# Attention and channel mix on one core: the table of ranks that sets the issue order, written anew

## The chip, the cores and the metric

The kernel runs on one core of a Trainium2 chip. The metric is the device time of the whole program in microseconds (us); lower is better. Five engines work side by side, each through its own queue in the order in which the program was written: TensorE (PE in the profile, with its weight loads as PEld), VectorE (DVE), ScalarE (ACT), GpSimd (POOL) and SyncE (SP), which here issues every DMA.

## The reference

Attention over 8 batches of 8 heads, 576 positions and 64 features per head, with a rotary turn of queries and keys; then a channel mix over the 512 joined features.

```
q_rot, k_rot = rotate(q), rotate(k)
attn = softmax(q_rot @ k_rot.T / sqrt(64))
x = attn @ v                                  # heads joined: 8 x 576 x 512
xk = mu_k * x + (1 - mu_k) * x_prev           # x_prev: one position earlier
xr = mu_r * x + (1 - mu_r) * x_prev
k = relu(xk @ w_k) ** 2                       # 512 -> 1024
out = sigmoid(xr @ w_r) * (k @ w_v)           # 1024 -> 512
```

## The kernel before

**Work.** The 64 heads go in 32 pairs (`PAIRS`, numbered 0 to 31 here; four pairs are one batch). For each pair the kernel loads queries, keys (`xq`, `xk`) and values. The rotary turn (`plan_rope`) is two multiplications by a table and a sum, on DVE or POOL (tiles `xq`, `xk`, line 276). For pairs 4 to 31 the result is split into a high part (`qh`, `kh`) and the rest (`ql`, `kl`), and a product is three matmuls (line 440); pairs 0 to 3, the early pairs, use one product in full precision. `plan_unit` makes scores in five column steps per pair, here written S9.2 for step 2 of pair 9: the products into PSUM (`scores`, two slots for pairs 4 to 31), a maximum on DVE (`nm`, L451), the exponential on ACT (`pe`, L461) and a transpose of 32x32 blocks on DVE (`p`, L466). `plan_move` sends `p` to DRAM (`turned`) and back (`rows`); the early pairs are transposed on PE instead (`turn`, L486, copied to `rows`). `plan_values` multiplies `rows` by the values (`av`, L558: 40 matmuls in the trace for a pair) and DVE divides by the sums into `xT` (L565, L570).

When four pairs of a batch are done, `plan_channel_mix` works on that batch in two halves of 288 positions. `plan_mix` makes eight mixed inputs: `mxf` on ACT and DVE (L615, L620), then `mxh` and `mxl`, its high part and rest. The products (`acc`, L644 to L646) are groups of three matmuls of 128x288: key products with `wk` (i runs over the four pairs of the batch), gate products with `wr`, value products with `wv` on the squared keys `kkh`, `kkl`. The weights arrive as 64-bit words in 20 blocks (`raw`) and are converted once on ACT, DVE and POOL (L317 to L330), with high parts and rests (`wk_h`, `wk_l`, ...).

**What sets the order.** Nothing is written out by hand. Each operation is handed to `Plan.op` with the engines that can do it, a cost for each, what it must come after, and a rank. `Plan.issue` plays the program through with its own costs: whenever an engine is free it takes, of the operations that are ready, the one of the smallest rank. The order that comes out is the order of each engine's queue on the chip, and the engine that took an operation is the one that does it. A rank is a place on a line plus an offset for its kind of work:

```
d, t = live[bg], PT * pi + (PB[pi] if pi < len(PB) else 0)
plan_unit(t + (EARLY_R if pi < EARLY else R)[f"u{c}"], d, c)
o = op("V", t + d["r"]["mx"] + 0.1 * x, dve(S), maximum, [m], [slots[x], s_m])
plan_channel_mix(b, 4 * PT * b + R["m0"] + MB[b], 4 * PT * (b + 1) + R["m0"] + MB[b])
heapq.heappush(ready[e], (now if e == "D" else ops[i][1] + ops[i][0][e][1], i))
```

`PT` is 18, so the 32 pairs lie 18 apart and the line is 576 long. `R` holds the offsets of all kinds (`EARLY_R` those of pairs 0 to 3), `PB` adds one for each of the first eight pairs, `MB` one for each batch of the channel mix. The `B_` numbers are added to the rank on DVE alone, where another engine could do the same operation (`B_ROPE` for rotary sums and multiplications, `B_LOW` for rests, `B_SPLIT` for high parts, `B_LOW_W` for rests of weights, and so on): a large positive one leaves the operation to the other engine.

Of the kernel before, what the change touches and what calls it, by code (L numbers as in the profile page):

```python
# [27 lines left out]
GROUPS = ((0, 1), (2, 3, 4))  # L28
WG = (128, 160)
EARLY = 4  # L30
R = dict(k=577.28, q=23.94, v=553.92, cs=313.3, mu=347.16, ld=3308.85, rope0=1037.47, rope1=2398.72, rope2=13.74,
         split0=4553.92, split1=-1190.14, u0=-627.56, u1=-590.7, u2=-98.62, u3=-1530.82, u4=-350.29, mx=-799.77,
         ex=-1615.41, tp=975.17, di=1063.67, dm=-166.72, da=-2593.89, dw=-1213.0, dr2=658.98, av=1791.79,
         ah=-71.03, nr=-1972.1, ev=-1476.18, m0=-73.47, mh=148.19, mk=-328.89, mr=920.2, ms=390.23, mx1=-169.36,
         mx2=-1161.49, mx3=-673.04, mg=17.09, mv=9.92, dr=-1173.42, key0=-2220.88, key1=1762.69, key2=159.56,
         gate0=1260.48, gate1=812.88, wk0=1007.96, wk1=1460.38, wr0=-387.66, wr1=-1396.89, wv0=-678.11, wv1=-664.42)
EARLY_R = dict(k=-559.86, q=-2227.6, v=-1071.07, ld=-3730.24, rope0=1705.02, rope1=1704.67, rope2=-667.21,
               split0=-2398.18, split1=3178.28, u0=483.09, u1=-4193.07, u2=-1556.07, u3=-996.5, u4=-1481.69,
               mx=1065.79, ex=626.39, tp=-3190.41, di=2732.73, dm=-985.63, da=-1413.1, dw=-1404.48, dr2=1968.8,
               av=-434.03, ah=988.45, nr=724.55, ev=-3038.47)  # L40
PB = (-4419.46, -975.52, -1700.76, -786.48, 770.77, -48.93, -486.06, 236.69)
B_COPY, B_ROPE, B_SPLIT, B_LOW, B_MIX, B_SQUARE, B_RELU, B_ROPE_E, B_SPLIT_W, B_LOW_W = -1799.5, -355.8, 2207.04, 1904.0, 2559.88, -962.11, -1190.36, -544.56, 1565.8, 1796.32
MB = (-221.65, -400.55, -193.51, -1944.88, 925.28, -1260.55, -180.2, -130.84)
CY = 12
SWITCH, STICK = (93, 220, 189), 20.0
BUFS = dict(nat=2, kh=2, kl=1, qh=2, ql=1, vs=1, pe=4, pe3=8, p0=1, p1=1, s=2, s3=3, nm=6, sums=2, rb=1, pt0=1, pt1=1, t=2, xT=5, raw=2, mxf=2, mxh=5, mxl=5, acc=2, hr=2, kkh=8, kkl=8, rt=3)
# [167 lines left out]
def rope_attention_channel_mix(ctx, tc, qt, kt, v, cs, mu, w_k, w_v, w_r, out):  # L214
# [182 lines left out]
    def plan_prep(t, b, g):  # L397
        d = live[b, g]
        d["r"] = EARLY_R if PAIRS.index((b, g)) < EARLY else R
        d["b"] = B_ROPE_E if PAIRS.index((b, g)) < EARLY else B_ROPE  # L400
# [94 lines left out]
    def plan_move(t, d):  # L495
# [309 lines left out]
```

## Time and profile before

| | us |
|---|---|
| runs | 957.88, 950.39, 954.88 |
| median of the runs | 954.88 |
| the profiled execution, first to last instruction | 949.7 |
| PE busy | 898.6 (95%) |
| DVE busy | 791.8 (83%) |
| ACT busy | 566.7 (60%) |
| POOL busy | 516.4 (54%) |

The profiled execution's own time is its span of 949.7 us; what lies around the span is not shown by the profile. Matmuls are pipelined, so a busy PE is one that always has a matmul under way. Moments are given in us from the start of the span.

### The profile page before, as it was taken

Reading aid. Unit: us, or ns where it says so; the run is one execution under the profiler, and the core shown is the slowest. Engines: PE = TensorE matmul, PEld = TensorE weight load, DVE = VectorE, ACT = ScalarE, POOL = GpSimd, SP = SyncE. Lnnn points to the kernel's source line nnn. Section 1 sums busy time; section 2 is a strip of 40 time slices with the busy share of each in tenths; the row PEclk is TensorE's granted clock in tenths of the full one; section 3 lists DMA queues with packets and bytes.
Section 4 is the critical chain, followed back from the end, with each engine's and each line's share of the span. In section 5 each row is a group of like instructions: output and inputs, shape, how many; then the busy total and the mean of one; then the engine's idle time right before and its main releaser. Section 6 shows DMA issues by size and latency. Waiting matters only on the chain.

```text
span 949.7 us, 18673 instructions
## 1 busy us (share of the span) xinstructions
PE 898.6 (95%) x6956; PEld 760.3 (80%) x6956; DVE 791.8 (83%) x1333; ACT 566.7 (60%) x1408; POOL 516.4 (54%) x516
## 2 busy tenths in 40 slices
PE   2778889999999999999999999999999999999998
PEld 1444578888688898887889888888889888788998
DVE  5799889899889989989989888898898889775652
ACT  3678877465566556655566646656576765525143
POOL 6668847664465656666554646385474845312201
PEclk9989999999999999999999999999999999999999
DMA  6555547999998988987788688898897699771000
GB/s 232 171 173 172 152 149 271 354 355 346 343 360 301 325 317 309 357 277 290 267 286 310 251 307 305 316 352 298 297 346 270 247 348 356 257 292 33 13 27 26
DMA packets 98107, 248.23 MB, mean 261 GB/s; under 512 B 11360, under 2 KB 43104, under 8 KB 90848
## 3 DMA queue, kind: packets, MB, share of 16 engines
q1 hardware_dynamic: 98016, 247.04, 73.4%
q8 instruction: 54, 0.88, 0.4%
q14 instruction: 37, 0.30, 0.1%
HBM read 154.47 MB, written 92.54 MB: 260 GB/s over the span
## 4 chain that ended last, share of the span: by engine, by line
PE 81%; DVE 8%; ACT 5%; DMA 3%; issue 2%; POOL 1%; SPq 0%; DVEq 0%; ACTq 0%; POOLq 0%
PE acc L644 19%; PE acc L645 16%; PE acc L646 16%; PE scores L440 15%; PE av L558 14%; DVE nm L451 3%; ACT early L461 1%; DVE p L466 1%; DVE pe L327 1%; PE turn L486 1%; DMA xk<-in_kt 1%; DMA raw<-in_w_k 1%; ACT pe L461 1%; DMA xq<-in_qt 1%; POOL pe L330 1%
## 5 line engine op out<-in xcount | busy, mean ns | idle before, releaser
L461 ACT ACTIVATE pe<-scores,nm 128x576 f32<-128x576 f32 x252 | 184.7, 738 | 106.0 <-DVE nm L451 105.3
L451 DVE TENSOR_REDUCE nm<-scores 128x1 f32<-128x576 f32 x288 | 205.4, 748 | 36.4 <-PE scores L440 35.0
L466 DVE STREAM_TRANSPOSE p<-pe 128x576 f32<-128x576 f32 x252 | 186.3, 760 | 6.1 <-ACT pe L461 5.0
L276 POOL TENSOR_TENSOR mxl<-mxf,mxh 128x288 fp32r<-128x288 f32 x101 | 87.4, 871 | 154.8 <-ACT mxh L280 107.2
L558 PE MATMUL av<-rows,values 128*64 128x320 f32 (+1 forms) x1280 | 162.3, 408 | 2.9 <-ACT rows L280 1.8
L644 PE MATMUL acc<-mxh,wk_h 128*128 128x288 f32 x512 | 158.3, 309 | 1.9 <-ACT mxh L280 1.3
L644 PE MATMUL acc<-kkh,wv_h 128*128 128x288 f32 x512 | 155.2, 303 | 1.6 <-DVE rt L700 1.6
L645 PE MATMUL acc<-mxl,wk_h 128*128 128x288 f32 x512 | 151.4, 296 | 0.5 <-POOL mxl L276 0.5
L646 PE MATMUL acc<-mxh,wk_l 128*128 128x288 f32 x512 | 151.4, 296 | 0.5 <-POOL wk_l L276 0.5
L645 PE MATMUL acc<-kkl,wv_h 128*128 128x288 f32 x512 | 150.9, 295 | 0.0
L646 PE MATMUL acc<-kkh,wv_l 128*128 128x288 f32 x512 | 150.8, 295 | 0.0
L558 PEld LDWEIGHTS av<-rows,values 128*64 128x64 f32 x1280 | 89.1, 137 | 63.8 <-issue 4.1
L440 PE MATMUL scores<-kh,qh 64*128 64x288 f32 (+1 forms) x648 | 108.3, 380 | 22.8 <-POOL qh L276 15.1
L276 POOL TENSOR_TENSOR kkl<-hr,kkh 128x288 fp32r<-128x288 f32 x97 | 88.0, 917 | 64.1 <-ACT kkh L280 36.6
L440 PEld LDWEIGHTS scores<-kh,qh 64*128 64x128 f32 (+1 forms) x648 | 61.9, 194 | 59.9 <-issue 25.2
L276 POOL TENSOR_TENSOR xq<-xq,turns 128x512 f32<-128x512 f32 (+1 forms) x83 | 79.3, 970 | 52.4 <-DMA xq<-in_qt 52.3
L644 PEld LDWEIGHTS acc<-mxh,wk_h 128*128 128x128 f32 x512 | 96.8, 189 | 12.6 <-issue 7.2
L644 PEld LDWEIGHTS acc<-kkh,wv_h 128*128 128x128 f32 x512 | 96.1, 188 | 10.0 <-issue 4.3
L645 PEld LDWEIGHTS acc<-mxl,wk_h 128*128 128x128 f32 x512 | 97.0, 190 | 0.7 <-POOL mxl L276 0.7
L646 PEld LDWEIGHTS acc<-mxh,wk_l 128*128 128x128 f32 x512 | 96.8, 189 | 0.7 <-POOL wk_l L276 0.7
L645 PEld LDWEIGHTS acc<-kkl,wv_h 128*128 128x128 f32 x512 | 96.3, 188 | 0.0
L646 PEld LDWEIGHTS acc<-kkh,wv_l 128*128 128x128 f32 x512 | 96.2, 188 | 0.0
(87 smaller groups left out, 1828.8 us busy)
## 6 DMA issues: line engine op xcount, KB each, us to landing
rows<-turned SPq DMA_DIRECT2D x28, 1600.0 KB, 10.3
turned<-p SPq DMA_DIRECT2D x28, 1440.0 KB, 8.6
rows<-turned SPq DMA_DIRECT2D x28, 1280.0 KB, 9.7
turned<-p SPq DMA_DIRECT2D x28, 1152.0 KB, 9.3
xq<-in_qt SPq DMA_DIRECT2D x32, 640.0 KB, 4.7
xk<-in_kt SPq DMA_DIRECT2D x32, 576.0 KB, 6.6
values<-in_v SPq DMA_DIRECT2D x32, 320.0 KB, 4.1
rb<-inv SPq DMA_DIRECT2D x64, 160.0 KB, 9.5
```

What stands on the lines that cost most here:

```text
L276: (V if e == "V" else G).tensor_tensor(out=out, in0=a, in1=b, op=op)
L327: V.scalar_tensor_tensor(out=word("m", U32), in0=d["low"], scalar=13, in1=word("m", U32), op0=ALU.logical_shift_right, op1=ALU.bitwise_or)
L330: G.tensor_tensor(out=word("m", I32), in0=word("m", I32), in1=word("e", I32), op=ALU.subtract)
L440: T.matmul(w[x][:, h, 0:H], lhsT=kind(d[q][r, c * P:(c + 1) * P]), rhs=kind(d[k][r, h * H:(h + 1) * H]), start=i == 0, stop=i == len(todo) ...
L451: V.tensor_reduce(out=w["nm", x], in_=w[x][:, :, 0:H], op=ALU.max, axis=AX.XY, negate=True)
L461: A.activation(w["p", x].rearrange("p (h n) -> p h n", h=2), w[x][:, :, 0:H], AF.Exp, bias=w["nm", x], scale=1.0, accum_out=d["sums"][:, u ...
L466: V.transpose(d["p", g][:, :, at:at + 32], w["p", x].rearrange("p (b n) -> p b n", n=32))
L486: T.transpose(a[i][0:n, k * P:(k + 1) * P], w["p", x][:, j * P:j * P + n], early["ident"])
L558: T.matmul(acc[(up, dn)[x], :, to:to + n], lhsT=d["vf"][:, 5 * x + j, :], rhs=rows_t[g][:, :, j, n * x:n * x + n], start=j == 0, stop=j == 4)
L644: T.matmul(w["a"], lhsT=w_h[:, i, sl], rhs=x["h"], start=(i == 0), stop=False)
L645: T.matmul(w["a"], lhsT=w_h[:, i, sl], rhs=x["l"], start=False, stop=False)
L646: T.matmul(w["a"], lhsT=w_l[:, i, sl], rhs=x["h"], start=False, stop=(i == count - 1))
```

## The change

The numbers of the table are replaced; nothing else of the program differs, except that the table takes one line less, so that every later line has a number lower by one (L644 becomes L643).

```
-R = dict(k=577.28, q=23.94, v=553.92, cs=313.3, mu=347.16, ld=3308.85, rope0=1037.47, rope1=2398.72, rope2=13.74,
-         split0=4553.92, split1=-1190.14, u0=-627.56, u1=-590.7, u2=-98.62, u3=-1530.82, u4=-350.29, mx=-799.77,
...
+R = dict(k=19.65, q=83.66, v=374.57, cs=-476.24, mu=387.97, ld=311.34, rope0=-48.99, rope1=-46.56, rope2=-21.37,
+         split0=503.76, split1=-142.69, u0=-71.23, u1=-171.73, u2=59.53, u3=11.22, u4=55.55, mx=-251.21, ex=-398.72,
...
-B_COPY, B_ROPE, B_SPLIT, B_LOW, B_MIX, B_SQUARE, B_RELU, B_ROPE_E, B_SPLIT_W, B_LOW_W = -1799.5, -355.8, 2207.04, 1904.0, 2559.88, -962.11, -1190.36, -544.56, 1565.8, 1796.32
-MB = (-221.65, -400.55, -193.51, -1944.88, 925.28, -1260.55, -180.2, -130.84)
+B_COPY, B_ROPE, B_SPLIT, B_LOW, B_MIX, B_SQUARE, B_RELU, B_ROPE_E, B_SPLIT_W, B_LOW_W = -172.58, 177.3, -225.73, -18.52, 402.78, 364.07, 62.33, 118.94, 962.24, -160.47
+MB = (9.62, 15.5, -50.38, -64.04, -67.79, -10.25, -467.09, 0.69)
```

The largest offset in `R` was 4553.92 and is 581.25; the line on which the pairs lie is 576 long, so an offset used to carry an operation past all pairs, and the new ones reach at most about as far as the line is long. What it does to the queues, at three places:

SyncE at the start of the program: `values` are the first pair's values, `turns` the rotary table, `raw` the weights. Before:

```order
1 L409 DMA values_87<-in_v 128x640
2 L726 DMA turns<-in_cs 128x1152
3 L362 DMA xk<-in_kt 128x2x576
4 L362 DMA xq<-in_qt 128x1280
5 L317 DMA raw<-in_w_r 128x2048 x2
6 L726 DMA mu_t<-in_mu 128x8
```

and with the change:

```order
1 L725 DMA turns<-in_cs 128x1152
2 L361 DMA xk<-in_kt 128x2x576
3 L361 DMA xq<-in_qt 128x1280
4 L408 DMA values_87<-in_v 128x640
5 L316 DMA raw<-in_w_v 128x2048 x2
6 L725 DMA mu_t<-in_mu 128x8
```

The values have moved behind the table, the keys and the queries, and the first weights are those of `w_v`, not of `w_r`.

PE behind the `av` product of pair 7, the last pair of batch 1; the two rows of scores are the end of S9.1, and a name such as `acc_930` is one PSUM accumulator. Before:

```order
914 L440 MATMUL scores_80<-kl,qh 128x288
915 L440 MATMUL scores_79<-kl,qh 128x288
916 L644 MATMUL acc_930<-mxh,wk_h 128x288
917 L645 MATMUL acc_930<-mxl,wk_h 128x288
918 L646 MATMUL acc_930<-mxh,wk_l 128x288
919 L644 MATMUL acc_931<-mxh,wk_h 128x288
```

and with the change:

```order
887 L439 MATMUL scores_80<-kl,qh 128x288
888 L439 MATMUL scores_79<-kl,qh 128x288
889 L643 MATMUL acc_959<-kkh,wv_h 128x288
890 L644 MATMUL acc_959<-kkl,wv_h 128x288
891 L645 MATMUL acc_959<-kkh,wv_l 128x288
892 L643 MATMUL acc_960<-kkh,wv_h 128x288
```

Before, batch 1's key products begin here at once; now value products of batch 0 stand between, eight groups of three before S9.2 and one after it. The first group that needs pair 7's own mixed input (i = 3) stood behind S9.1, six groups and S9.2; now behind S9.1, eight groups, S9.2 and five groups.

DVE at the division of pair 7 (`xT`); `mxf` is the mixed input made from it, `xk` are keys of pair 10, the maxima `nm` are those of S9.1. Before:

```order
285 L276 TENSOR_TENSOR xq<-xq,turns 128x512 x2
286 L276 TENSOR_TENSOR xk<-xk,turns 128x576
287 L451 TENSOR_REDUCE nm<-scores_80 128x1
288 L451 TENSOR_REDUCE nm<-scores_79 128x1
289 L565 TENSOR_TENSOR xT<-av,rb 128x4x2x32 x2
290 L570 TENSOR_TENSOR xT<-av,rb 64x64 x2
291 L276 TENSOR_TENSOR xk<-xk 128x576
292 L620 SCALAR_TENSOR_TENSOR mxf<-xT,mu_t,mxf 128x288
```

and with the change:

```order
272 L465 STREAM_TRANSPOSE p<-pe 128x18x32 x2
273 L275 TENSOR_TENSOR xk<-xk,turns 128x576
274 L564 TENSOR_TENSOR xT<-av,rb 128x4x2x32 x2
275 L569 TENSOR_TENSOR xT<-av,rb 64x64 x2
276 L450 TENSOR_REDUCE nm<-scores_80 128x1
277 L450 TENSOR_REDUCE nm<-scores_79 128x1
278 L619 SCALAR_TENSOR_TENSOR mxf<-xT,mu_t,mxf 128x288
```

The division has moved ahead of the two maxima, the two query multiplications and the key sum have left this place, and one multiplication of pair 10's keys still stands in front.

## Rows read from the trace of the kernel before

**Rows 1.** The page, part 1: busy us, share of the span, instructions of each engine.

```profile
PE 898.6 (95%) x6956; PEld 760.3 (80%) x6956; DVE 791.8 (83%) x1333; ACT 566.7 (60%) x1408; POOL 516.4 (54%) x516
```

**Rows 2.** Stretches: length, busy us of PE, PEld, DVE, ACT, POOL, clock, DMA, GB/s.

```profile
15.00:73.00 58.00, 44.54 (x226) 27.23 (x226) 48.53 (x72) 40.63 (x94) 41.88 (x38) 0.91 0.54 173
73.00:118.00 45.00, 36.81 (x250) 23.83 (x252) 41.89 (x67) 36.71 (x84) 38.04 (x30) 1.00 0.58 171
118.00:132.00 14.00, 11.05 (x80) 7.97 (x79) 12.15 (x22) 10.34 (x24) 3.86 (x6) 0.88 0.28 108
...
150.00:237.00 87.00, 85.28 (x692) 72.23 (x693) 78.17 (x130) 52.90 (x136) 54.57 (x52) 1.00 0.94 332
237.00:257.00 20.00, 17.77 (x133) 14.05 (x130) 16.30 (x28) 12.58 (x32) 10.18 (x10) 0.91 0.96 348
257.00:300.00 43.00, 42.14 (x341) 35.28 (x338) 38.99 (x67) 28.05 (x74) 28.64 (x29) 1.00 0.97 359
300.00:500.00 200.00, 199.23 (x1594) 170.19 (x1592) 179.98 (x297) 120.47 (x306) 116.30 (x118) 1.00 0.84 298
500.00:800.00 300.00, 299.49 (x2408) 258.66 (x2406) 263.94 (x440) 187.75 (x476) 170.51 (x173) 1.00 0.85 306
```

**Rows 3.** Timeline, start of the program: start, us, engine, line, [idle before <- what ended it].

```profile
0.74 0.39 SPq L409 DMA_DIRECT2D values<-in_v  x1
1.18 0.42 SPq L726 DMA_DIRECT2D turns<-in_cs  x1
...
8.26 0.76 DVE L276 TENSOR_TENSOR xk<-xk,turns 128x576 f32<-128x576 f32 x1 [7.39 <-DMA xk<-in_kt]
...
13.17 1.85 POOL L276 TENSOR_TENSOR qh<-xq 128x640 f32<-128x640 f32 x1 [0.29 <-DVE xq L276]
```

**Rows 4.** Timeline behind pair 7's av product.

```profile
231.91 0.58 SPq L362 DMA_DIRECT2D xk<-in_kt  x1
...
239.11 0.53 PE L440 MATMUL scores<-kh,qh 64*128 64x288 f32 x4
...
240.51 0.76 DVE L276 TENSOR_TENSOR xk<-xk,turns 128x576 f32<-128x576 f32 x1 [2.40 <-DMA xk<-in_kt]
...
241.18 1.42 DVE L451 TENSOR_REDUCE nm<-scores 128x1 f32<-128x576 f32 x2
...
242.51 0.75 DVE L565 TENSOR_TENSOR xT<-av,rb 128x256 f32<-128x256 f32 x2
...
244.65 0.51 DVE L620 SCALAR_TENSOR_TENSOR mxf<-xT,mu_t,mxf 128x288 f32<-128x288 f32 x1
...
245.94 0.40 PE L644 MATMUL acc<-mxh,wk_h 128*128 128x288 f32 x1 [1.31 <-ACT mxh L280]
```

**Rows 5.** Line 276 up to 277 us, by tile: count, ns min/median/max.

```profile
L276 POOL TENSOR_TENSOR xq<-xq,turns x30: 445/908/1711, 10.2 to 267.2; 128x128 f32<-128x128 f32 x17, 128x512 f32<-128x512 f32 x13
...
L276 DVE TENSOR_TENSOR xq<-xq,turns x18: 245/737/1685, 9.8 to 262.2; 128x512 f32<-128x512 f32 x11, 128x128 f32<-128x128 f32 x7
```

**Rows 6.** Groups by line over the whole span: busy us, mean ns of one.

```profile
L276 POOL TENSOR_TENSOR xq<-xq,turns 128x512 f32<-128x512 f32 (+1 forms) x83 | 79.3, 970 | 52.4 <-DMA xq<-in_qt 52.3
...
L276 DVE TENSOR_TENSOR xq<-xq,turns 128x512 f32<-128x512 f32 (+1 forms) x45 | 37.5, 849 | 1.6 <-DMA xq<-in_qt 1.5
...
L276 DVE TENSOR_TENSOR ql<-xq,qh 128x640 fp32r<-128x640 f32 x16 | 23.2, 1450 | 0.0
...
L276 DVE TENSOR_TENSOR xk<-xk 128x576 f32<-128x576 f32 x10 | 11.7, 1173 | 0.8 <-POOL xk L276 0.7
...
L276 DVE TENSOR_TENSOR wk_l<-pe,wk_h 128x512 fp32r<-128x512 f32 x4 | 4.8, 1194 | 0.8 <-ACT wk_h L280 0.6
```

**Rows 7.** Tile mxf from 118 to 300 us: one form of DVE, ns min/median/max.

```profile
L620 DVE SCALAR_TENSOR_TENSOR mxf<-xT,mu_t,mxf x27: 474/550/1715, 126.2 to 297.7; 128x288 f32<-128x288 f32 x27
```

**Rows 8.** PE's timeline, from value products into scores and back.

```profile
232.18 0.29 PE L645 MATMUL acc<-kkl,wv_h 128*128 128x288 f32 x1
232.32 0.29 PE L646 MATMUL acc<-kkh,wv_l 128*128 128x288 f32 x1
232.54 0.53 PE L440 MATMUL scores<-kh,qh 64*128 64x288 f32 x4
...
233.53 0.40 PE L644 MATMUL acc<-kkh,wv_h 128*128 128x288 f32 x1
```

More of the change, by code (lines that the diff above doesn't have):

```diff
@@ L30 @@
 EARLY = 4
-R = dict(k=577.28, q=23.94, v=553.92, cs=313.3, mu=347.16, ld=3308.85, rope0=1037.47, rope1=2398.72, rope2=13.74,
-         split0=4553.92, split1=-1190.14, u0=-627.56, u1=-590.7, u2=-98.62, u3=-1530.82, u4=-350.29, mx=-799.77,
[L33 to L41, printed above, removed]
-B_COPY, B_ROPE, B_SPLIT, B_LOW, B_MIX, B_SQUARE, B_RELU, B_ROPE_E, B_SPLIT_W, B_LOW_W = -1799.5, -355.8, 2207.04, 1904.0, 2559.88, -962.11, -1190.36, -544.56, 1565.8, 1796.32
@@ L43 @@
-MB = (-221.65, -400.55, -193.51, -1944.88, 925.28, -1260.55, -180.2, -130.84)
+R = dict(k=19.65, q=83.66, v=374.57, cs=-476.24, mu=387.97, ld=311.34, rope0=-48.99, rope1=-46.56, rope2=-21.37,
+         split0=503.76, split1=-142.69, u0=-71.23, u1=-171.73, u2=59.53, u3=11.22, u4=55.55, mx=-251.21, ex=-398.72,
+         tp=18.58, di=499.55, dm=-479.01, da=-144.37, dw=-322.09, dr2=244.03, av=237.69, ah=-73.55, nr=132.55,
+         ev=105.56, m0=129.5, mh=-5.93, mk=-43.11, mr=-30.14, ms=1.57, mx1=7.69, mx2=228.59, mx3=18.5, mg=0.55,
+         mv=-6.41, dr=-233.37, key0=581.25, key1=258.8, key2=-6.65, gate0=-400.9, gate1=-288.81, wk0=39.8, wk1=135.26,
+         wr0=528.39, wr1=165.76, wv0=21.03, wv1=29.52)
@@ new lines @@
+EARLY_R = dict(k=227.71, q=-27.31, v=-429.13, ld=-298.19, rope0=-337.18, rope1=136.44, rope2=-12.73, split0=-319.12,
+               split1=-469.77, u0=-22.72, u1=-610.98, u2=283.69, u3=103.88, u4=75.61, mx=-76.95, ex=-240.36, tp=198.0,
+               di=52.88, dm=-34.61, da=-32.29, dw=496.44, dr2=189.69, av=-120.17, ah=-199.01, nr=-373.05, ev=102.6)
+PB = (-475.64, -354.4, -178.07, 94.77, -48.86, 55.63, -78.3, -180.9)
+B_COPY, B_ROPE, B_SPLIT, B_LOW, B_MIX, B_SQUARE, B_RELU, B_ROPE_E, B_SPLIT_W, B_LOW_W = -172.58, 177.3, -225.73, -18.52, 402.78, 364.07, 62.33, 118.94, 962.24, -160.47
```

## The prediction, made before the changed kernel ran

> **What bounds the kernel now.** I began with the page's busy shares: PE is busy 898.6 of 949.7 us [rows 1], so at most 51 us stand open whatever the order, since the change adds and removes no matmul. Then I cut the span into stretches, to see where those 51 us lie [rows 2]. From 300 to 800 us PE is idle 0.77 + 0.51 = 1.3 us of 500: there only PE's own work counts, and no order can gain anything beyond fewer changes between kinds of product. Up to 15 us PE has nothing at all. From 15 to 118, the early pairs, PE is idle 13.5 + 8.2 = 21.7 us, and DVE is busy 48.5 of 58 and then 41.9 of 45 us: DVE (with its maxima, rotary turns and conversion of weights) is the engine that ends the waits. From 118 to 300 PE is idle again in pieces: 2.95, 1.7, 2.2 and 0.9 us, with DVE at 84 to 91% and the DMA engines at 94 to 97% from 150 on; between 132 and 150 it was never idle. [...] Last I looked into the largest of these holes, behind pair 7's av product [rows 4]. So the change is worth what it does before 300 us.
>
> **The change part by part.** All sums are made against the profiled execution, 949.7 us; the median of the runs, 954.9, lies 5.2 above it, and I add that at the end.
>
> *Start.* DVE waits until 8.26 for the first keys, behind the issue of the values at 0.74 and of the table at 1.18 [rows 3]. Moving the values back saves 0.44 us of SyncE and takes their transfer out of the way. DVE's and POOL's first rotary work is dealt out anew too: POOL now gets two multiplications of 128 columns for one of 512 and one of 128, and the sum `qh`, which at 13.17 + 1.85 released the first scores [rows 3], should start some 0.8 us sooner by the difference between POOL's longest and median xq multiplication (1.71 and 0.91 us [rows 5]). That makes 1.2 us, of the range from 0.4 to 1.7. Nothing hides it: from there to 118 us one thing leads to the next.
>
> *Early pairs.* Counted in the two queues up to what pair 3's av product needs, DVE has 132 operations before and 133 now: it loses 11 rotary operations and gains eight rests of weights. At the means of their groups that is nothing (under 0.1 us); POOL gains 4 us. Since POOL was busy 38.0 of 45 us in that stretch [rows 2] I charge a part of it, 1.0 us, between 0 and 3.
>
> *Pairs 4 to 9.* Up to what pair 9's av product needs (it began at 277 us), DVE's queue holds 357 operations before and 346 now. Of its xq multiplications 18 [rows 5] become 5, which is 13 x 0.849 = 11.0 us less; four rotary sums fewer, 4 x 1.17 = 4.7 less; against that six more rests of weights, at most 6 x 1.194 = 7.2, and three more `ql`, 3 x 1.45 = 4.4 [rows 6]. With the small kinds it is some 8 us less work for DVE, at the same place of PE's order. POOL takes them: 13 more xq multiplications, 13 x 0.970 = 12.6 us [rows 5, 6], and with the rest about 13 more.
>
> *The hole behind pair 7.* Pair 7's av product ends at 239.1, when S9.1 begins; the first group with pair 7's mixed input starts at 245.94, that is 6.8 us later, by way of a DVE that stood 2.40 us for pair 10's keys (their DMA was issued at 231.91), then did two maxima, the division at 242.51 and the mix at 244.65 [rows 4]. What PE had in hand meanwhile was S9.1 (0.99 us from scores to the next product), six groups of three at 0.13 to 0.14, so 0.4 each, and S9.2 [rows 8]: 0.99 + 2.4 + 0.99 = 4.4 us. With the change it is 0.99 + 3.2 + 0.99 + 5 x 0.40 = 7.2 us, and the division stands ahead of the maxima. The hole closes: 2.2 us of idle time in 237 to 257, and 0.09 x 20 = 1.8 us of clock [rows 2], 4.0 together. If pair 10's keys come later than now, DVE still stands in front of the division and half of it stays.
>
> *The other holes from 118 to 300.* The one behind pair 3's av product (118 to 132) has the same form, but here the change puts the first groups with pair 3's input ahead of S4.2, so that PE has less in hand, while the mix comes ahead of the maxima: I take nothing for it, between a loss of 1 and a gain of 4.6 (2.95 idle and 0.12 x 14 of clock). Of 1.7 + 0.9 us in the remaining stretches I take half, 1.3, for the 8 us less in front of DVE.
>
> *Changes of product.* A group follows a group after 0.14 us, scores after 0.22 [rows 8]. Such steps from products into scores or av are 145 before and 139 now: 6 x 0.09 = 0.5 us less.
>
> *After 300 us.* The end of PE's queue, the last batch's channel mix, has the same order; DVE has the 8 us to do later, where it is busy 88 to 90% [rows 2] and PE does not wait for it: nothing, within 2 us either way.
>
> Sum: -1.2 + 1.0 - 4.0 - 1.3 - 0.5 = -6.0, so 943.7 for the profiled execution and 948.9 beside the median, say 949.
>
> **A rule that speaks against it.** Mixing on DVE takes 0.474 us at the least and up to 1.715 [rows 7], the same form on the same data: a DVE instruction with two inputs in SBUF is held up when POOL is at work. [...]
>
> **The rivals.** (1) POOL slows DVE. Up to 277 us DVE and POOL were busy together long enough that what POOL gains could be taken from DVE: 13 - 8 = 5 us later at pair 9 in place of earlier, the start's gain eaten by the early pairs and the hole behind pair 7 only moved: 959.9, and with two more holes of 4 us each 968. It decides from the point where POOL's extra work falls into stretches in which DVE is already above 90%, as in 73 to 118. For it speaks the row of the mix; against it that POOL was busy 54.6 of 87 us in 150 to 237 and that DVE's maxima, transposes and reads of PSUM are most of its work. (2) The DMA engines bound this stretch. They were busy 94 to 97% from 150 to 300 at 332 to 359 GB/s [rows 2], and the bytes that pair 9 needs are the same in both orders. Then PE's hole comes back as a wait for rows or keys; start and changes of product alone remain, -1.7: 953.2. Against it: PE had no wait for rows, and the hole at 242 was made by one load in a queue. (3) All holes go: start -1.7, idle 118 to 300 -7.8, clock -3.5 of which I count half, product changes -0.5: -11.7, 943.1. For it speaks that a DVE with 8 us less to do is ahead everywhere. (4) The change doesn't do what it says: offsets of 400 to 960 still cross most of the line, the queues are alike over hundreds of rows, and the time stays at 954.9.
>
> **How the numbers follow.** Forecast 0.40, at 949; (3) 0.26 at 943; (2) and (4) 0.20 at 953 to 955; (1) 0.14 at 960. The range runs from 939 (the sum with the far ends of start, early pairs and the pair 3 hole: -0.5 - 1.0 - 4.6 - 1.3 more than forecast, with 2 us of noise) to 960, the nearer price of (1). One per cent of the median, 9.5 us, is about what a measurement of this kernel can tell from no change: the bounds are 945.3 and 964.4. Faster: nearly all of (3) and a fifth of the forecast, 0.32; slower: the far half of (1) and a little of (4), 0.08; within: 0.60.
>
> **What would show it.** The first scores before 14.5 us; pair 3's av product begins between 115 and 120; PE idle under 1 us and the clock at 1.00 for the 20 us behind pair 7's av product; pair 9's av product begins near 271; PE idle under 2 us from 300 to 800. [...]

## The result, and the profile after

The changed kernel takes 940.8 us (median of four runs, 936.31 to 941.4) where the kernel before takes 954.5: a ratio of 0.9852, with a 95% interval of 0.981 to 0.9893, so 13.7 us or 1.4% less. The forecast was 949 with a range of 939 to 960. The range holds the time; the likeliest case does not, and the time lies below 945.3, on the side called faster, which had a chance of 0.32. The profiled execution of the changed kernel is one of 941.4 us with a span of 939.6.

The page of the changed kernel, part 1: busy us, share of the span, instructions of each engine.

```profile
PE 894.2 (95%) x6956; PEld 758.8 (81%) x6956; DVE 768.8 (82%) x1344; ACT 566.6 (60%) x1407; POOL 511.6 (54%) x506
```

DVE is busy 23 us less than in [rows 1], with 11 instructions more. PE has the same 6956 matmuls.

Stretches of the changed kernel: length, busy us of PE, PEld, DVE, ACT, POOL (instructions), clock, DMA, GB/s.

```profile
15.00:73.00 58.00, 45.75 (x260) 27.14 (x258) 48.97 (x76) 42.21 (x96) 47.34 (x41) 0.91 0.56 186
73.00:118.00 45.00, 35.17 (x214) 22.70 (x210) 36.80 (x58) 32.73 (x77) 32.79 (x27) 0.89 0.44 140
118.00:132.00 14.00, 10.69 (x71) 7.16 (x72) 11.46 (x21) 10.87 (x25) 8.01 (x9) 0.82 0.26 82
...
150.00:237.00 87.00, 86.50 (x713) 72.38 (x711) 74.33 (x127) 56.58 (x145) 56.98 (x56) 1.00 0.98 347
237.00:257.00 20.00, 19.77 (x158) 16.42 (x154) 16.53 (x32) 12.61 (x33) 16.16 (x17) 1.00 0.99 353
257.00:300.00 43.00, 41.46 (x334) 35.88 (x331) 38.28 (x61) 29.37 (x76) 27.50 (x26) 1.00 0.93 337
300.00:500.00 200.00, 199.72 (x1617) 171.77 (x1617) 177.75 (x308) 124.01 (x314) 115.95 (x113) 1.00 0.87 312
500.00:800.00 300.00, 300.00 (x2427) 260.77 (x2428) 262.24 (x469) 183.39 (x466) 163.97 (x166) 1.00 0.85 303
```

Read against [rows 2]. From 237 to 257 the hole is gone: idle 0.23 us for 2.23, clock 1.00 for 0.91. From 73 to 132 this execution is worse than that of before: the clock is 0.89 and 0.82 where it was 1.00 and 0.88. And from 300 to 800 PE is busy 499.72 us where it was busy 498.72, one microsecond more of 500; but look at the number of its matmuls in the same stretch, 1617 + 2427 = 4044 for 1594 + 2408 = 4002. At 500 / 4044 = 0.124 us each, 42 more matmuls are 5.2 us of progress that the busy share does not show.

Where the gain stands along the program, as the moment at which the same piece of work begins on PE, before and after:

| work | before | after | difference |
|---|---|---|---|
| first scores | 15.1 | 13.8 | -1.3 |
| S3.0 | 84.0 | 79.0 | -5.0 |
| pair 2's av product | 97.6 | 97.1 | -0.5 |
| pair 3's av product | 117.8 | 118.8 | +1.0 |
| pair 7's av product | 234.1 | 231.1 | -3.0 |
| pair 9's av product | 277.2 | 275.7 | -1.5 |
| first key product of batch 1, half 1 | 302.4 | 300.4 | -2.0 |
| the same of batch 4, half 1 | 624.9 | 618.3 | -6.7 |
| the same of batch 7, half 1 | 912.9 | 902.8 | -10.1 |

The rows of pairs 7 and 9 compare unequal work. Ahead of pair 7's av product PE now has nine groups of value products less, the ones that moved behind it (9 x 0.40 = 3.6 us), and ahead of pair 9's three groups more (1.2 us). At equal work the two rows read +0.6 and -2.7, so some 3 us are won between them, where the hole was.

Two things were not foreseen: in these two executions five microseconds are won by 84 us and lost again by 98, and eight of the ten at the end are won behind 302 us, where the prediction had nothing.

The start in the timeline of the changed kernel, beside [rows 3].

```profile
0.74 0.38 SPq L725 DMA_DIRECT2D turns<-in_cs  x1
...
7.99 0.76 DVE L275 TENSOR_TENSOR xk<-xk,turns 128x576 f32<-128x576 f32 x1 [7.12 <-DMA xk<-in_kt]
...
11.80 1.94 POOL L275 TENSOR_TENSOR qh<-xq 128x640 f32<-128x640 f32 x1
...
13.79 1.81 PE L439 MATMUL scores<-kh,qh 64*128 64x288 f32 x6 [13.79 <-POOL qh L275]
```

The first keys are there 0.27 us sooner and the sum `qh` begins 1.37 us sooner. Behind pair 7's av product, beside [rows 4]:

```profile
236.08 0.53 PE L439 MATMUL scores<-kh,qh 64*128 64x288 f32 x4
...
236.51 0.76 DVE L275 TENSOR_TENSOR xk<-xk,turns 128x576 f32<-128x576 f32 x1 [2.12 <-issue]
...
237.18 0.75 DVE L564 TENSOR_TENSOR xT<-av,rb 128x256 f32<-128x256 f32 x2
...
239.79 0.60 DVE L619 SCALAR_TENSOR_TENSOR mxf<-xT,mu_t,mxf 128x288 f32<-128x288 f32 x1
...
242.57 0.29 PE L643 MATMUL acc<-mxh,wk_h 128*128 128x288 f32 x1
```

DVE still stands 2.12 us ahead of the multiplication of pair 10's keys, but the division follows S9.1's start after 1.1 us, not 3.4, and PE comes to batch 1's first products at 242.57 without a gap.

Line 275 up to 275.7 us by tile, and the mix on DVE from 118 to 300, beside [rows 5, 7]: count, ns min/median/max.

```profile
L275 POOL TENSOR_TENSOR xq<-xq,turns x43: 450/904/1752, 10.0 to 270.4; 128x128 f32<-128x128 f32 x22, 128x512 f32<-128x512 f32 x21
...
L275 DVE TENSOR_TENSOR xq<-xq,turns x5: 452/936/1043, 9.5 to 195.8; 128x512 f32<-128x512 f32 x3, 128x128 f32<-128x128 f32 x2
```

```profile
L619 DVE SCALAR_TENSOR_TENSOR mxf<-xT,mu_t,mxf x28: 469/520/1448, 126.5 to 298.5; 128x288 f32<-128x288 f32 x28
```

POOL has its 13 more multiplications and DVE its 13 fewer; the mixes on DVE are no slower for it (639 ns on the mean for 770).

### The profile page after: what moved, and what is told of

It is laid out like the page before. It is cut to its first block, busy times and chain, and to the rows that moved or that the text cites. A ratio compares the mean times of both kernels' runs of the same rounds, so it can differ in the third digit from the quotient of the medians.

```text
span 939.6 us, 18611 instructions
## 1 busy us (share of the span) xinstructions
PE 894.2 (95%) x6956; PEld 758.8 (81%) x6956; DVE 768.8 (82%) x1344; ACT 566.6 (60%) x1407; POOL 511.6 (54%) x506
## 4 chain that ended last, share of the span: by engine, by line
PE 82%; DVE 5%; DMA 4%; ACT 4%; POOL 4%; issue 1%; SPq 0%; DVEq 0%; POOLq 0%; ACTq 0%
PE acc L643 19%; PE acc L644 17%; PE acc L645 17%; PE scores L439 14%; PE av L557 13%; DMA raw<-in_w_v 2%; DMA xk<-in_kt 2%; ACT early L460 1%; DMA xq<-in_qt 1%; PE turn L485 1%; DVE nm L450 1%; POOL xq L275 1%; POOL xk L275 1%; POOL pe L329 1%; ACT pe L323 1%
## 5 line engine op out<-in xcount | busy, mean ns | idle before, releaser
L643 PE MATMUL acc<-mxh,wk_h 128*128 128x288 f32 x512 | 157.8, 308 | 1.0 <-ACT mxh L279 0.8
L643 PE MATMUL acc<-kkh,wv_h 128*128 128x288 f32 x512 | 154.0, 301 | 0.8 <-DVE rt L699 0.4
L275 POOL TENSOR_TENSOR mxl<-mxf,mxh 128x288 fp32r<-128x288 f32 x86 | 74.0, 862 | 145.6 <-ACT mxh L279 73.1
L644 PE MATMUL acc<-mxl,wk_h 128*128 128x288 f32 x512 | 151.6, 296 | 0.5 <-POOL mxl L275 0.5
L644 PE MATMUL acc<-kkl,wv_h 128*128 128x288 f32 x512 | 151.0, 295 | 0.0
L275 POOL TENSOR_TENSOR kkl<-hr,kkh 128x288 fp32r<-128x288 f32 x94 | 83.7, 900 | 102.6 <-ACT kkh L279 75.8
L439 PE MATMUL scores<-kh,qh 64*128 64x288 f32 (+1 forms) x648 | 107.3, 381 | 18.8 <-POOL qh L275 13.8
L643 PEld LDWEIGHTS acc<-mxh,wk_h 128*128 128x128 f32 x512 | 96.8, 189 | 10.6 <-issue 8.3
L643 PEld LDWEIGHTS acc<-kkh,wv_h 128*128 128x128 f32 x512 | 96.2, 188 | 6.8 <-issue 4.3
L275 POOL TENSOR_TENSOR xq<-xq,turns 128x128 f32<-128x128 f32 (+1 forms) x99 | 94.4, 968 | 8.7 <-DMA xq<-in_qt 8.5
L275 POOL TENSOR_TENSOR xk<-xk,turns 128x576 f32<-128x576 f32 x47 | 73.4, 1574 | 46.8 <-DMA xk<-in_kt 44.9
L644 PEld LDWEIGHTS acc<-mxl,wk_h 128*128 128x128 f32 x512 | 97.0, 189 | 1.1 <-POOL mxl L275 1.1
L644 PEld LDWEIGHTS acc<-kkl,wv_h 128*128 128x128 f32 x512 | 96.2, 188 | 0.0
```

The source lines that it names most:

```text
L275: (V if e == "V" else G).tensor_tensor(out=out, in0=a, in1=b, op=op)
L439: T.matmul(w[x][:, h, 0:H], lhsT=kind(d[q][r, c * P:(c + 1) * P]), rhs=kind(d[k][r, h * H:(h + 1) * H]), start=i == 0, stop=i == len(todo) ...
L643: T.matmul(w["a"], lhsT=w_h[:, i, sl], rhs=x["h"], start=(i == 0), stop=False)
L644: T.matmul(w["a"], lhsT=w_h[:, i, sl], rhs=x["l"], start=False, stop=False)
```

## The experiments

**The theories.** A: most of the gain lies behind 300 us, in short waits of PE that its busy share hides. PE has two accumulators for the channel mix. A product that opens one has to wait until DVE or ACT has emptied it, and in the order before such a product stands, in 24 places behind 300 us, at 1.0 us of PE work or less behind the last product of the accumulator's former use; after, in 8. Such a place in the timeline of the kernel before:

```profile
623.82 0.29 PE L646 MATMUL acc<-kkh,wv_l 128*128 128x288 f32 x1
...
624.21 0.29 PE L646 MATMUL acc<-kkh,wv_l 128*128 128x288 f32 x1
...
624.43 0.81 DVE L700 TENSOR_TENSOR rt<-acc,rt 128x288 f32<-128x288 f32 x2
...
624.93 0.40 PE L644 MATMUL acc<-mxh,wk_h 128*128 128x288 f32 x1 [0.42 <-DVE rt L700]
```

The first half's last value product but one ends with the matmul at 623.82, and only one group, the last value product, stands between it and the next half's first key product, which needs its accumulator. The multiplication by the gate that empties the accumulator begins at 624.43, and the key product comes 0.72 us after the matmul ahead of it, where the step from one matmul to the next is 0.13. In that trace the three openers at 0.4 us were late by some 0.4 us on the mean, and those at 1.2 us by 0.01 or less. B: the gain is made before 300 us and only kept.

For runs that change the order itself, the five queues are written out as one list, and `Plan.issue` hands out that list in place of playing the ranks through:

```
-        while True:
-            for e, queue in ready.items():
...
+        todo = [(int(c) // 8, "TVAGSD"[int(c) % 8]) for c in codes]
+        while todo:
+            for n, (i, e) in enumerate(todo):
+                if deps[i] <= done and free(i):
+                    break
...
+            ops[i][3](e)
```

Such kernels have the line numbers of the kernel before. With the list of the kernel after unchanged, the time is that of the kernel after:

> The kernel after, its five queues written out as a list in place of the planner's table; no instruction differs or stands elsewhere. Every theory expects the time of the kernel after, 941 us (939 to 943). It is the base for the runs that are edits of such a list.

Measured: 941.54 us (937.32 to 945.53) beside 954.02, ratio 0.9865 (0.9823 to 0.9906). The list is a fair base.

**Where the gain lies: two orders spliced.** At the first key product of batch 1, half 1, the two orders have issued the same work but for two operations, so one can take over from the other there.

```
 head = order_1[:cut]
+order = head + [x for x in order_2 if x not in head]
```

> The order of the kernel before up to the first key product of batch 1, half 1 (it began at 302 us), and from there on, on every engine, the order of the kernel after. Theory A (most of the gain lies after 300 us, in short waits of PE for an accumulator or a score slot that a busy PE hides): the stretch behind the cut is 8 us shorter, the one ahead of it as before; 946.4 us (944 to 949), against 954.5 before and 940.8 after. Theory B (the gain is made before 300 us, by the start, the early pairs and the hole behind pair 7, and the rest only keeps it): 953 us (951 to 955).

Measured: 944.93 us beside 953.08, ratio 0.9918 (0.9893 to 0.9943): 8.2 us less, with the head of before (302.8 us at the cut, 302.4 before). From 300 to 800 it has 1611 + 2423 = 4034 matmuls:

```profile
300.00:500.00 200.00, 199.30 (x1611) 171.26 (x1610) 177.21 (x310) 121.39 (x308) 114.38 (x113) 1.00 0.86 305
500.00:800.00 300.00, 300.00 (x2423) 260.95 (x2423) 262.08 (x469) 184.26 (x466) 163.60 (x164) 1.00 0.85 303
```

> The mirror: the order of the kernel after up to the first key product of batch 1, half 1 (300 us there), the order of the kernel before behind it. Theory A: the head gives its 2 us and the irregular order behind it loses its 8 us again, 952.5 us (950 to 954). Theory B: 942 us (940 to 944). If the two parts are independent, the gains of this run and of the first one add up to the 13.7 us of the whole change within 2 us.

Measured: 952.17 us, ratio 0.9977 (0.9949 to 1.0004): 0.9 us less than before by the medians, 2.2 by the ratio. In its profiled run the cut comes at 299.0 us, 3.4 ahead of before, and what is behind it takes 646.4 us where it took 644.0. Both runs speak for A and against B. The traces agree: from that key product to PE's last matmul it is 635.4 to 636.9 us in eight traces with the order of after there (the kernel after, the first splice and six of the other runs), and 644.0 and 646.4 in the two with the order of before. The two gains make 9 to 10 us, not the 12.5 to 13.7 of the whole within 2 as expected: some 3 us stay unassigned. The head alone scatters by more than that: with the queues of after up to the cut, four traces reach it at 297.4, 299.0, 300.4 and 303.2 us, three with the queues of before at 302.4 to 302.9.

**The mechanism: near and far.** First the places are spread in the order before:

```
 PE, one of 30 places
-L644 to L646  acc_930<-kkh,wv_h ...
 L440          scores_80<-kh,qh ...    (12 matmuls)
+L644 to L646  acc_930<-kkh,wv_h ...
```

> The kernel before, with the queues of DVE, ACT, POOL and SP unchanged; on PE alone, behind 290 us, 30 products are exchanged with a neighbour, so that a product that opens an accumulator stands at least 1.2 us of PE work behind the last product of the accumulator's former use (24 stood at 1.0 us or less, 2 do now; of the score slots the nearest goes from 0.8 to over 2.3 us). Theory A: the openers at 1.0 us or less cost 6.1 us in the trace of before; some 5 of these go, 949.5 us (947.5 to 952). Rival C (PE waits because DVE and ACT stand in another order, with DVE held up by the gates; where the products stand on PE doesn't matter): 954.5 us (953 to 956).

Measured: 952.72 us, ratio 1.0003 (0.9971 to 1.0035). Nothing, where A had 5 us. Its trace shows that the waits were moved and not taken away: 1585 + 2399 = 3984 matmuls from 300 to 800. The worst, in the timeline of this run:

```profile
445.47 0.45 ACT L695 ACTIVATE rt<-rt 128x288 f32<-128x288 f32 x1
...
446.12 1.65 DVE L620 SCALAR_TENSOR_TENSOR mxf<-xT,mu_t,mxf 128x288 f32<-128x288 f32 x1
...
446.52 0.29 PE L646 MATMUL acc<-kkh,wv_l 128*128 128x288 f32 x1
...
447.69 1.41 DVE L451 TENSOR_REDUCE nm<-scores 128x1 f32<-128x576 f32 x2
...
449.02 0.44 DVE L700 TENSOR_TENSOR rt<-acc,rt 128x288 f32<-128x288 f32 x1
...
449.52 0.40 PE L644 MATMUL acc<-mxh,wr_h 128*128 128x288 f32 x1 [1.53 <-DVE rt L700]
```

The gate is ready at 445.92 and the product's last matmul ends at 446.81, but the multiplication stands in DVE's queue behind a mix and two maxima, and comes at 449.02. In the order before, PE had waited 0.42 us at this place. So the distance on PE alone is not what decides; it is how DVE's and ACT's queues stand against PE's. I call this A2.

Then the other way: the order after, made crowded.

```
 PE, one of 29 places: last product of the accumulator's former use
+L644 to L646  the product that opens it again
 one other group (0.4 us)
-L644 to L646  the product that opens it again
```

> The kernel after, all other queues unchanged; on PE alone, between 300 and 800 us, 29 products that open an accumulator are moved ahead of their neighbour, so that only one group of three (0.4 us) lies between them and the last product of the accumulator's former use; only one stood so near. Theory A: 0.41 us for each, as the three of that distance cost in the trace of before, so 12 us: 953 us (948 to 956). Rival C (the place on PE doesn't matter): 941 us (940 to 943).

Measured: 952.72 us, ratio 0.9991 (0.9968 to 1.0015): 11 to 13 us more than the kernel after, as A worked out, though DVE, ACT, POOL and SP have the same queues. PE's weight loads waited for these most in this run, from 300 to 939 us (engine, line, waited for: us, times, longest; waits put down to `issue` left out):

```profile
PEld acc L644 <- ACT hr L661: 4.8, 12, 0.6
PEld acc L644 <- DVE rt L700: 3.9, 10, 0.4
PEld acc L644 <- ACT rt L691: 3.1, 9, 0.3
```

These are 31 waits for the three operations that empty an accumulator (the relu, the value's multiplication, the gate's first exp), 0.38 us each. Read off the matmuls (the step onto an opener and the one behind it, less the medians of such steps), the 30 openers at 0.4 us (the 29 and one that stood so before) are late by 0.42 us each on the mean, 12.6 us together; the stretch behind 302 us is 14.5 us longer than in the kernel after. From 300 to 800 it has 1574 + 2374 = 3948 matmuls, 96 fewer than the kernel after, which is 11.9 us, while PE is busy 494.32 us, only 5.4 less than there: less than half of the loss shows as idle time.

**One rank out of step.**

```
-... mv=-6.41, dr=-233.37, key0=581.25, ...
+... mv=-6.41, dr=-1173.42, key0=581.25, ...
```

> The kernel after with one entry of its table put back: dr = -1173.42 in place of -233.37, the rank of the four operations that empty an accumulator (the relu of a key, the exp of a gate, the multiplication and the output of a value). Theory A2 (what counts is how the queues of DVE and ACT stand against PE's, so that the operation that empties an accumulator is there when its last product ends): one rank in a class of its own again takes these operations out of step and brings waits back over the whole steady part: 955 us (948 to 962), most of the 14 us behind 300 us. Rival D (the gain is that of the whole order and one rank is worth little): 942 us (940 to 945).

Measured: 955.12 us beside 952.76, ratio 1.0027 (1.0008 to 1.0047). One entry of 102 costs the whole gain, in the size that A2 gave. The place is another: the first key product of batch 3, half 1 (512.5 us in the kernel after) is 16.5 us late, and the last one of all, batch 7, half 1, is 16.6 us late. The loss lies ahead of 530 us and not "over the whole steady part"; the rest of the order found its step again. More than half of it is made ahead of 302 us: the first key product of batch 1, half 1 comes 5.3 us late (305.7), and four products of scores, some 4 us, which stand ahead of it in the kernel after, are then still to do. In the first of these rows PE is idle 2.9 us, at a clock of 0.83:

```profile
237.00:257.00 20.00, 17.08 (x117) 13.13 (x117) 15.15 (x28) 9.39 (x24) 6.77 (x8) 0.83 0.94 344
...
300.00:500.00 200.00, 196.62 (x1573) 166.49 (x1570) 173.85 (x291) 122.81 (x314) 118.61 (x119) 0.99 0.89 317
```

```
-... gate0=-400.9, gate1=-288.81, ...
+... gate0=1260.48, gate1=812.88, ...
```

> The kernel after with gate0 and gate1 (the two later ACT steps of a gate, which the multiplication of a value needs) put back to 1260.48 and 812.88, late by some 1.3 us. Theory A2: the queues of the gates have slack in this order, PE's order stays nearly the same, 941 us (940 to 943). Rival E (DVE stands at the value's multiplication for its gate, 9.5 us in two waits in the trace of before, and this is what PE paid for): 946 us or more.

Measured: 946.82 us, ratio 0.9939 (0.9917 to 0.996), some 5 us more than the kernel after. A2 as I used it was wrong here, and E has the size, but its way is not to be seen: from 300 to 360 us DVE stands at a value's multiplication for a product of PE (1.2 us, as in the kernel after), never for a gate. Between 300 and 357 us this run falls 3.7 us behind the kernel after, and behind that no more. There DVE has the same queue in both. At 330 us it runs 0.66 us late, and a rest, which begins 0.13 us behind a multiplication on POOL, takes 1.60 us where it took 0.42; the maxima come 1.9 us late and PE waits for an exponential. In DVE's and PE's timelines of this run:

```profile
330.36 1.60 DVE L275 TENSOR_TENSOR mxl<-mxf,mxh 128x288 fp32r<-128x288 f32 x1
...
336.40 1.41 DVE L450 TENSOR_REDUCE nm<-scores 128x1 f32<-128x576 f32 x2
```

```profile
338.06 0.40 PE L439 MATMUL scores<-kh,qh 64*128 64x288 f32 x1 [1.31 <-ACT pe L460]
```

Behind that wait the clock is 0.91 on the mean from 340 to 360 us, which is 1.8 us more. How the gates' ranks set this off is open.

**The head: what bounds the early pairs.**

```
 mostly DVE and ACT, one of 28 places
-a step of the conversion of weights (L321 to L330)
 the maximum or exponential of an early pair
+a step of the conversion of weights (L321 to L330)
```

> The kernel after with 27 operations moved one to three places ahead in their queues before 128 us, and one at 262 us: nine maxima, exponentials and rotary steps on DVE and ACT ahead of a step of the conversion of weights or a copy, the division of pairs 1 and 3 and some conversion steps likewise, two PE operations and one of POOL. From 128 us on the order is that of after. Theory F (the early pairs are a chain through DVE and ACT in which conversion of weights stands in the way, and what is won there is kept): 934 us (931 to 937), with pair 3's av product begun near 112. Rival 2 of the prediction (the DMA engines, busy 98% from 150 to 257 us, bound the stretch behind): pair 3's av product comes sooner, the first key product of batch 1, half 1 doesn't (300 us), and the time stays at 940 us.

Measured: 943.84 us, ratio 0.9898 (0.9872 to 0.9924): nothing gained on the kernel after (941.54 as a list). Pair 3's av product begins at 118.7, as in the kernel after: neither theory has it right, since rival 2 let it come sooner too. DVE is busy 4.4 us less from 15 to 73 us, and PE no sooner. What stayed is the clock, 0.89 from 73 to 118 and 0.80 from 118 to 132.

```
-            nc.sync.dma_start(rows_t[g].rearrange(...), src)
+            nc.sync.dma_start(rows_t[g][:, 0:(1 if 4 <= pi <= 9 else 4)].rearrange(...), src[:, 0:(1 if 4 <= pi <= 9 else 4)])
```

> The kernel after, every queue as it is, but the loads of `rows` of pairs 4 to 9 bring a quarter of their columns (the output of these pairs is not computed). It takes 12 transfers from 2.9 MB to 0.7 MB a pair out of the stretch from 120 to 280 us. Rival 2 of the prediction (DMA engines bound the stretch): pair 9's av product begins at 270 us or sooner in place of 275.7, and the time falls to 935 us or less. Theory A2 (PE's own work and its waits for accumulators fill that stretch): 940.5 us (939 to 942), pair 9's av product within 1.5 us of 275.7.

Measured: 940.44 us, ratio 0.9871 (0.9841 to 0.99); pair 9's av product at 275.3. The DMA engines fall from 98% to 77%, and PE's share stays:

```profile
150.00:237.00 87.00, 86.50 (x708) 73.01 (x709) 78.74 (x130) 57.44 (x147) 59.88 (x58) 1.00 0.77 257
237.00:257.00 20.00, 20.00 (x164) 16.64 (x162) 16.91 (x31) 13.01 (x33) 13.98 (x15) 1.00 0.74 266
```

Rival 2 is out for the changed kernel: DMA engines that are 98% busy did not bound this stretch.

**The hole behind pair 7, put back.**

```
 PE
 S9.0
+nine groups of value products of batch 0, half 1
 pair 7's av product, S9.1
-eight groups of value products of batch 0, half 1
 S9.2
-one group of value products of batch 0, half 1
 DVE
-L565, L570  xT<-av,rb   (pair 7's division)
 L451        nm<-scores  (the two maxima of S9.1)
+L565, L570  xT<-av,rb
```

> The kernel after with the place behind pair 7's av product put as it was before: on PE the nine products of values that stand behind pair 7's av product and S9.1 go ahead of them, so that only S9.1, groups of the next half and S9.2 are left in hand behind it, and on DVE the four divisions of pair 7 go behind the two maxima of S9.1. The prediction's own step gave 4.0 us for this hole: 945 us (944 to 947), the first key product of batch 1, half 0 later by some 4 us and all that follows with it. Rival G (the products have only changed places, and what is lost there is won back up to 300 us): 941 to 942 us.

Measured: 945.66 us beside 941.54 for the list unchanged: 4.1 us by the medians, 5.8 by the ratios, 0.9926 and 0.9865, whose intervals (0.9898 to 0.9953, 0.9823 to 0.9906) just overlap. But the hole is not the one of before:

```profile
237.00:257.00 20.00, 16.16 (x121) 13.29 (x119) 13.02 (x23) 10.68 (x27) 11.63 (x14) 0.91 0.87 317
```

```profile
244.74 0.40 PE L440 MATMUL scores<-kh,qh 64*128 64x288 f32 x1 [3.51 <-ACT pe L461]
```

PE is idle 3.84 us, where it was 2.23. In the order before, six groups stood between S9.1 and S9.2, and PE waited 1.31 us for pair 7's mixed input [rows 4]; here S9.2 stands right behind S9.1 and waits 3.51 us for the exponential that frees its slot. So the run shows what a gap at this place costs, and not the old hole itself. The traces give that: from pair 7's av product to the first key product of batch 1, half 1, PE's work differs between the orders only by the nine groups. Six traces with the queues of after there take 66.1 to 69.3 us, three with those of before 70.1 to 71.9 with 3.6 us for the nine groups added, this run 71.4 with the same added. Between the means of the six and the three lie 4.1 us. (The moment at which batch 1's first key product begins does not show it: 246.6 in this run, 242.6 in the kernel after, 247.8 in the list unchanged.)

**The clock in the early pairs.** PE's timeline in the kernel after shows where in this execution the five microseconds of the early pairs went:

```profile
88.16 0.77 PE L485 MATMUL turn<-early 128*128 128x128 f32 x5 [0.81 <-DVE rows L281]
89.50 1.33 PE L485 MATMUL turn<-early 128*128 128x128 f32 x5 [0.57 <-ACT rows L279]
...
93.57 1.33 PE L485 MATMUL turn<-early 128*128 128x128 f32 x5 [1.07 <-ACT rows L279]
94.83 2.29 PE L439 MATMUL scores<-kh,qh 64*128 64x288 f32 x8
```

From 89 us on the same five transposes take 1.33 us in place of 0.77, and the granted clock is 0.68, 0.50 and 0.54 from 88 to 100 us. PE alone in four-microsecond pieces (length, busy us, clock, DMA, GB/s), in the kernel after:

```profile
84.00:88.00 4.00, 2.86 (x17) 1.00 0.56 172
88.00:92.00 4.00, 2.92 (x14) 0.68 0.79 287
92.00:96.00 4.00, 2.93 (x14) 0.50 0.71 227
96.00:100.00 4.00, 4.00 (x22) 0.54 0.50 152
```

The profiled execution of the kernel before has 1.00 in all four. That is no property of its order, though: the first splice, which has that order here, shows the same fall at the same place:

```profile
84.00:88.00 4.00, 3.19 (x19) 1.00 0.59 172
88.00:92.00 4.00, 3.47 (x13) 0.69 0.65 201
92.00:96.00 4.00, 3.54 (x14) 0.50 0.76 264
```

The spread run, the third with the order of before here, has 0.93, 0.50 and 0.50 in these pieces. Of the twelve traces without extra work for PE, eleven have the clock below full somewhere from 84 to 104 us (from 73 to 118 us it is 0.89 to 0.92 on the mean in the kernel after, the list unchanged and five other runs), and that of before is the one that has not. With the order of before, S3.0 begins at 82.2 to 84.0 us in the three traces and pair 3's av product at 117.8 to 118.8; in the nine others at 78.4 to 83.0 and at 117.9 to 121.8. So the clock takes its part in both orders.

What it costs is tried by giving PE work that nobody needs, in the places where it waits:

```
-                for k, j in enumerate(js):
-                    T.transpose(a[i][0:n, k * P:(k + 1) * P], w["p", x][:, j * P:j * P + n], early["ident"])
+                for k, j in [(1, 0), (2, 1), (3, 2)][:1 * i] + list(enumerate(js)):
+                    T.transpose(a[i][0:n if k < len(js) else P, k * P:(k + 1) * P], w["p", x][:, j * P:j * P + (n if k < len(js) else P)], early["ident"])
```

> The kernel after with one more transpose by PE in each of the 36 short turns of the early pairs, into columns of their own PSUM tile that nobody reads (no result changes): 36 times 0.13 us, some 5 us more work for PE, spread over the places from 17 to 118 us where it stands idle for 22 us. Theory H (the granted clock eats what the early pairs gain: 0.68, 0.50 and 0.54 from 88 to 100 us in the trace of after, 1.00 there in that of before; a PE that is idle less keeps the clock): clock 0.95 or more in 73 to 118, pair 3's av product at 116, 938 us (936 to 940). Rival I (the early pairs are bound by the chain through DVE, ACT and POOL, and the clock is no part of it): 941 to 943 us, pair 3's av product at 118 to 120.

Measured: 939.6 us (938.23 to 946.89), ratio 0.9858 (0.9815 to 0.99); pair 3's av product at 116.1, clock 0.97 from 15 to 73 and 1.00 from 73 to 118. By the time alone it can't be told from the kernel after.

With `[:3 * i]` in place of `[:1 * i]`:

> As the run before with three such transposes for each short turn, 108 in all, some 14 us more work for PE. Theory H: the clock at 1.00 in most of 15 to 118, pair 3's av product at 115 or sooner, 937 us (934 to 941). Rival I: the work lies on the chain in part, pair 3's av product at 122 or later and 945 us or more.

Measured: 937.41 us (936.74 to 938.63), ratio 0.982 (0.9781 to 0.9859), the fastest of all; 4.1 us less than the kernel after as a list. The intervals of the two still overlap. Pair 3's av product at 116.0. In the stretches (columns as above):

```profile
15.00:73.00 58.00, 49.53 (x326) 32.20 (x324) 50.17 (x78) 42.02 (x96) 48.87 (x41) 1.00 0.55 189
73.00:118.00 45.00, 37.59 (x280) 27.02 (x278) 38.99 (x59) 35.20 (x80) 34.71 (x28) 1.00 0.47 150
```

There are 108 more matmuls, and PE is done with the early pairs 2.8 us sooner than in the kernel after. Pair 3's av product begins at 116.1 and 116.0 in the two runs, ahead of all twelve traces without extra transposes. Theory H holds at this place, where the clock is part of the path, and I does not; that the whole time gains by it is likely and not shown.

## Why the prediction was right or wrong

**What failed: "from 300 to 800 us PE is idle ... 1.3 us of 500: there only PE's own work counts, and no order can gain anything", and with it the term "after 300 us: nothing, within 2 us either way".** The order is worth 8.2 us there (the head of before with the rest of after). The row was read rightly and does not say what I took from it. In the rows a matmul of 0.29 us begins 0.13 to 0.14 us behind the one ahead of it [rows 8], and a late one leaves only a part of its delay as a gap: in the crowded run 11.9 us of progress were lost from 300 to 800 us and 5.4 us showed as idle time. The number of matmuls from 300 to 800 us tells it: 4002 before, 4044 after, 4034 with the head of before and the rest of after, and 3981, 3984 and 3948 where the rest is that of before, spread, or crowded. The rows of before, [rows 2], held 1594 + 2408 matmuls and a weight load busy 428.85 us of 500 before the run, and I did not ask how many would fit. The busy time of the weight loads goes with that number: from 300 to 800 us it is 0.107 us a matmul in the traces of before, after, both splices, the spread and the crowded run. From before to after PEld goes from 428.85 to 432.54 us, 0.9% more for 1.0% more matmuls, while PE goes from 498.72 to 499.72, 0.2% more.

That the range holds the time is therefore luck: its low end, 939, was made of far ends of the start, the early pairs and the hole behind pair 3 with 2 us of noise, and none of these far ends came, while the term that was worth 8.2 us stood in the sum as nothing.

What brings the waits is shown in part. From the cut on, the trace of before is 8.0 us longer than that of after. I set each step from one matmul to the next against the median of such steps in the kernel after and add up what is over: 4.6 of the 8.0 us lie at the products that open an accumulator, 2.6 at the products of scores, 0.4 at other groups, and 0.4 come from more changes of product. So the accumulators are the larger part and not the whole. That an opener 0.4 us behind its accumulator's last use costs 0.4 us is shown by the crowded order. That spreading the openers on PE is not enough is shown by the spread one. The one rank put back shows that the rank of the operations that empty accumulators is worth the whole gain in this table; as more than half of that loss lies ahead of 302 us, it does not show that waits for accumulators are the way. Which of the old ranks put the queues of DVE and ACT out of step with PE behind 300 us is not settled: it would take the old table's entries one by one, and each entry changes the whole play.

**Start, -1.2: right.** -1.3, the first scores at 13.8.

**Early pairs, +1.0: near in the number by luck, wrong in the reason.** Pair 3's av product came 1.0 later in the profiled executions, but not by POOL's work: POOL is busy 80.1 us from 15 to 118, where it was 79.9. The new order ran 5.0 us ahead at S3.0 and lost it while the granted clock was 0.50 to 0.68 from 88 to 100 us; the execution of before that it is compared with has 1.00 there, and others of its order have not. The two runs with extra transposes begin pair 3's av product 2.7 and 2.8 us sooner. The prediction priced the clock in two stretches and took it for full in the early pairs, since it was so in the one execution that it read.

**Pairs 4 to 9 and rival (1), POOL slowing DVE: the counts right, the rival wrong.** 18 multiplications on DVE became 5 and 30 on POOL 43; the mix's median fell from 550 to 520 ns [rows 7]. From 15 to 300 us DVE is busy 242.0 us for 252.8 and POOL 199.3 for 190.2, so the work moved as forecast, though the terms that the prediction lists add up to 4.1 us of its 8. (DVE's share in 237 to 257 was also 82%, below the 84 that the prediction gives as the least.) That DVE's mixes take longer while POOL is at work is seen in the trace of before: over the whole span the 60 mixes of the form in [rows 7] with no POOL instruction beside them take 0.47 to 0.52 us, the 68 with one 0.47 to 1.83, 0.91 at the median; its ten rests `mxl` without take 0.41 to 0.46, the 17 with 0.41 to 1.05; the maxima of 576 columns take 0.71 to 0.76 either way. But the 9.1 us more on POOL did not lengthen the mixes. Pair 9's av product was forecast near 271 and began at 275.7, some 1.2 us of it by three groups more ahead of it: most of what DVE was spared did not come out on PE.

**The hole behind pair 7, -4.0: right.** 4.1 us at equal work between the traces with and without it, with both parts as forecast: idle time 0.23 us for 2.23, clock 1.00 for 0.91. The run with a hole put back there loses 4.1 to 5.8 us, but by a larger hole with another wait. **The hole behind pair 3, 0:** right, it is still there (idle 3.31 us of 14, clock 0.82). **The other holes, -1.3:** 0.5 in sum; from 150 to 237 PE is idle 0.50 us where it was 1.72, from 257 to 300 it is 1.54 where it was 0.86. **Changes of product, -0.5:** too small to be told apart.

**Rival (2), the DMA engines:** refuted for the changed kernel: with a quarter less traffic from 150 to 257 us the time and pair 9's av product stay. **Rival (3)** gave 943.1, near the time, for a reason that is not the one: the holes behind pair 3 and in 73 to 118 did not go. **Rival (4):** refuted.

Start, hole and the part behind 300 us make 1.3 + 4.1 + 8.2 = 13.6 us, which is the whole. But the head alone (the second splice) is worth 0.9 to 2.2 us where start and hole would make 5.4, and the head's four traces lie 2.7 us ahead of the three of before on the mean, so the parts add up only within some 4 us, and the even sum is partly luck.

## What to carry to other kernels

A stretch in which PE is "busy 99.7%" need not be at PE's limit: count the matmuls that a microsecond brings, and the busy share of the weight loads, before calling an order worthless there. With two PSUM accumulators, as here, look at what PE has to do between the last product of one use and the first of the next: 0.4 us was too little, 1.2 us enough where the operation that empties the accumulator came in time. Spreading the products on PE alone gained nothing, so look at the places of those operations on DVE and ACT too; to move these alone was not tried. Where an early stretch full of short waits has a granted clock below full, as here (0.89 from 73 to 118 us), some products that nobody reads, put where PE waits, can cost less than the clock does: here they won 2.7 us at pair 3. And compare several executions before giving a difference of a few microseconds in such a stretch to the order.

## What the runs showed of the hardware

The clock fell in the kernel after although no wait of PE from 84 to 95 us was longer than 1.07 us; PE was busy 2.86 of 4 us ahead of the fall. In the kernel before it was busy 3.18 and 2.91 of 4 us there and the clock stayed at 1.00; in the first splice, with the same order, it was busy 3.19 of 4 us and the clock then fell to 0.69 and 0.50. So the same queues kept the clock in one execution and lost it in another. With the 108 extra transposes the clock is 1.00 from 15 to 73 and from 73 to 118 us, in the kernel after 0.91 and 0.89.

The scatter between runs goes with this clock: six runs of the kernel after as a list lie between 937.32 and 945.53 us at a mean granted clock of 0.982 to 0.989, six with the 108 transposes between 936.74 and 938.63, each at 0.996.

A wait was followed by more than its own length: with the gates late, 1.31 us of waiting at 338 us are followed by 20 us at a mean clock of 0.91, where the kernel after has 1.00; 0.09 x 20 is 1.8 us more.

A rest of 128x288 on DVE took 1.60 us in one run and 0.42 in another at the same place of the same queue, 0.13 and 0.05 us behind the start of the same multiplication on POOL. What decided on the 1.2 us no run shows.
